# Gated sum of attention and a channel MLP: maxima's pieces, square roots, first weights and the order of units are moved

## The chip, the cores and the metric

The kernel runs on one core of a Trainium2 chip. The metric is device time in microseconds of one launch; smaller is better. The engines are TensorE (PE for its matmuls, PEld for its weight loads), VectorE (DVE), ScalarE (ACT), GpSimd (POOL) and SyncE (SP, which only issues DMAs). ACT issues some DMAs too, in its own instruction stream; in the profile "ACTq" and "SPq" are the DMA-issuing instructions of these two.

## What is computed

```python
def _A_ref(x, wqkv, wo):          # S=2048, D=512, H=32 heads of 16, window W=256
    q, k, v = split(x @ wqkv)
    scores = q @ k.T * (Dh ** -0.5)              # per head
    scores = where(0 <= i - j < W, scores, -1e9)
    return (softmax(scores) @ v) @ wo

def _B_ref(x, w1, b1, w2, b2):    # F=1792
    y = (x - mean(x)) / sqrt(var(x) + 1e-5)
    return gelu(y @ w1 + b1) @ w2 + b2

g = sigmoid((x * gate_w).sum(-1, keepdims=True))
out = g * _A_ref(A_x, A_wqkv, A_wo) + (1 - g) * _B_ref(B_x, ...)
```

In the kernel both branches start from arrays of the inputs given; everything is float32. Matmuls are made of two parts each: a value is split into a high part (rounded to the type fp32r) and a low part (the difference), and three products are summed: high by high, high by low, low by high.

## The kernel before, in words

The work has three stages.

**First stage: projections (the loop over `units`, 48 of them).** A q/k unit (`qk_unit`, matmuls on L288) makes 128 rows of q or k for 512 tokens in 12 matmuls; a v unit (`v_unit`, L313) makes v for 128 tokens in 12 matmuls, four by each of the three products. `first_units` makes the first two q/k units (L275) while their weights and inputs arrive in pieces. After a q/k unit, `qk_out` copies the result with ACT (a high part), subtracts it on DVE (a low part, L119, the helper `lo_part`), and both parts are written to DRAM: the high part by DMAs that ACT issues (L298), the low part by SP one step later (L299). Results of units sit in four PSUM buffers `d`.

Each unit is one step. `plan` holds what is put ahead of which unit: `at(n, fn)` puts `fn` ahead of unit n, and `after(k, fn)` defers to k steps later (`tick` runs these first). In the plan are, among others: the split of the weights Wv (`load_wv`; unit 6 is the first that needs it), the split of x chunk 3 (ahead of unit 6, its low parts on POOL), the weights of the next groups of heads (`load_w`: loaded at one step, split three steps later by an ACT copy and a DVE subtraction), the loads of stacks (below), and the statistics of the MLP branch: `stat_unit` loads 128 rows of x with SP (L434) and three steps later takes mean, variance and the gate's dot product on DVE (L438 to L440); `stat_end` (ahead of units 22 and 30, for half of the tokens each) takes 1/sqrt(var + eps) by an integer first guess and four Newton steps on [128, 8] tiles (L451 to L458), transposes the result (L461) and stores it to DRAM (L462). `load_y` reads it back (L481), loads x transposed (L489), and normalises on POOL (L492, L493: two operations of 128x512 for each of eight pieces).

**Maxima and attention.** q and k of four heads are loaded back as "stacks" (`load_stacks`, L324, two DMAs of 196 KB for 256 tokens; stack p holds heads 4p to 4p+3 in two pairs). An S unit (`s_pair`, L337) makes scores of a pair of heads for 128 queries, and DVE takes each query's maximum (L346 copies the masked block, L347 reduces). After four blocks of queries the maxima of both pairs are put back into the stacks as extra rows, so that the second product subtracts them. This way (`put_max`) has four pieces: `parts` (POOL splits into high and low part, L358 and L119), `turn` (DVE transposes, L362), `put` (SP stores to a DRAM tile `md`, L365), `rest` (SP loads them into the rows of `qk`, L371, which waits for the store's landing). A T unit (`st_pair`, L392) makes scores transposed for 128 keys, ACT takes exp (L394), POOL masks (L396). A P unit (`pv`, L411) multiplies by v.

**Second stage: attention and the MLP's first product, by the written order.** `ORDER` is a string of 1202 letters. T, S and P run the next unit of their kind; f runs the next two matmuls of the MLP's first product (`fill`, L611, no dependence on attention). The string is written out by a planner beforehand; the kernel only follows it. `spot[0]` counts the letters. In this stage the four pieces of a group's maxima are issued at `CHAIN` letters after the S unit that ends the group: (6, 11, 13, 20). In the first stage they follow by steps instead. A T unit at an even block of keys also issues the load of the next stack (`block`). Scores, P results and MLP results share four pairs of PSUM banks in turn (`two`, `ring`).

**Third stage: output.** The MLP's second product (`mlp2`, L821), the attention's output projection (L800) and the gates g0 and g1, which are exp, plus one, reciprocal (L466 on ACT, L470 and L471 on DVE, at the end of `stat_end(1)` in the kernel before).

Every engine runs its instructions in program order, and an instruction that waits holds those behind it. DMAs are issued by SP in program order too.

Of the kernel before, what the change touches and what calls it, by code (L numbers as in the profile page):

```python
# [13 lines left out]
F32R = mybir.dt.float32r  # L14
# [3 lines left out]
ALU = mybir.AluOpType  # L18
# [6 lines left out]
DT = D // 128  # L25
KT = D // 64
# [8 lines left out]
EPS = 1e-5  # L35
NEG = -3.0e38
U8 = mybir.dt.uint8
ORDER = ("fTSTffffffSffTfSfffTfSffTfSfffTSffffSPffSfffTSfffTfSffTfSfffTfffTSfTfffSffSPTTSPTSfffTfSffTfSfffTSff"
         "fTfSfffTSfffTfTfffSPSTTPfTSfTfffSffTfSfffTSfffTfSfffTfSffSPfSffSPfTfTSffTfSfffTSfffTfSffTfSfffTSfffT"
         "ffSfSPTSTPSTSPTSTfffSfTSfffTfSPTSffTffTfSffTfSfffTSffTfffSTPSTSPSTfTfffTSffTffSffTSffffTSfffTfSfffTS"  # L40
         "fffSPSTSPTTSTSPSfffTSfffTfSffTfTfffSffTfSfffTSfffTfSfPSTSPTSfSfffTffSffTfSfTffSffTfSfffTSfffTfSffSPS"
         "TSPfTfTSfffTfffTSfTfffSffTfSfffTSfffTfSffSPSTSPfTfSfTffSfffTSfffTffTffTSffTfSfffTfSffSPSTSPTffTSffTf"
         "fSffTfSfffTSfffTffTfSfTfffSfTPSfSPTTSPTfSfffTSfffTfSffTfSfffTSfffTfSffTfSfffSPTTSPSTffSfffSPTfSTfffT"
         "ffTSffTffTffTSffTfTfffSfSPTSTffTffTSffTffSffSPTfSfTffSfffTSfffTffSfTPfSTPSTSPfSTfffTfSfTffSffTfSfffT"
         "SfffTfSffTfSfffSPSTTPfTSfTfffSffTSffffTSfffTfSfffTffTfSfffSPSTSPfTffTfTSfffTfSffTfSfffTSfffTfSffTfSf"
         "ffSPTSPSfffTSfffTfSffTfSfffTSfffTfSfffSffSTffPTSSPfSfffTSfffTfSffTfSfffTSfffTfSffTfSfffSPTSffTffTffT"
         "SffTffTfSPfTSPTSffTffTffTSffTfSfffSPSTTPfTSfTfffSffTSffffTSffPfTSffTffSffTSffffSPSfTfSffffSTfffTffST"
         "fffTfSfTffSffTfSfffSPSTSPfTffTSffTfffTfSfTffSfffTSffffTSffffTSfPSTSPffTfTfSffTfffTfTSffffTSffTfSfffT"
         "SfffSfPTSTPTSPSffTSfffTfTffSfTffSfffTfSfffTSfffTffSfSPTfffTTPTffTfTfffTTfPfTTPTffTfTfffTfTffTfPfTTPf"
         "TT")  # L50
LAG = 6
CHAIN = (6, 11, 13, 20)


@with_exitstack
def gated_mix_kernel(ctx, tc: tile.TileContext, xt, x2, wqk, wv, wo, xa, gw, w1, w2, b1, b2, out):
    nc = tc.nc
    dve, act, pool, pe, sp = nc.vector, nc.scalar, nc.gpsimd, nc.tensor, nc.sync
# [18 lines left out]
    def get(key, tag, bufs, shape, dt=F32):  # L77
        return left[key].tile(list(shape), dt, name=nm(tag), tag=tag, bufs=bufs)
# [3 lines left out]
    def t2(dt=F32, shape=(128, 512)):  # L82
        return get("work", "t", nt[0], shape, dt)
# [28 lines left out]
    def view(t, *ap, off=0):  # L112
        return bass.AP(tensor=t.tensor, offset=t.offset + off, ap=[list(x) for x in ap])

    def f32(t):
        return t.bitcast(F32)

    def lo_part(lo, src, hi, eng=dve):
        eng.tensor_tensor(out=lo, in0=src, in1=f32(hi), op=ALU.subtract)  # L119

    def copy(dst, src):
        act.activation(dst, src, AF.Copy)  # L122
# [4 lines left out]
    def after(k, fn):  # L127
        todo.setdefault(step[0] + k, []).append(fn)
# [17 lines left out]
    stat = dram.tile([2, 2, S // 2], F32, name="stat")  # L146
# [12 lines left out]
    g0 = consts.tile([128, NB], F32, name="g0")  # L159
    g1 = consts.tile([128, NB], F32, name="g1")  # L160
    mv = consts.tile([128, NB, 2], F32, name="mv")
    rt = consts.tile([128, 2, 2, NB // 2], F32, name="rt")
# [14 lines left out]
    def split(w, raw, both=False):  # L177
        if both:
            dve.tensor_copy(w[:, 0], raw)
        else:  # L180
            copy(w[:, 0], raw)
        lo_part(w[:, 1], raw, w[:, 0])
# [29 lines left out]
    def load_wv(dt):  # L212
        w, raw = get("work", "wv", DT, (128, 2, 512), F32R), t2()
        wvs.append(w)
        sp.dma_start(raw, wv[dt])
        return lambda: split(w, raw)

    def load_x(c):
        h, l = x8(), x8()
# [20 lines left out]
        return rest, hi, lo  # L240

    def first_units():
        ws, raws, os = [], [], []
        for t in range(2):
            w = wt()
            wq[0, t] = w
            ws.append(w)
            raws.append(t2())
        pieces = (slice(0, 128), slice(128, 256), slice(256, 512))
        for k in pieces:  # L250
            for t in range(2):
                act.dma_start(raws[t][:, k], wqk[0, t, :, k])
        _, hi, lo = load_x(0)
        idle = t2()
        dve.memset(idle, 0.0)
        idle = idle.bitcast(BF16)
        o = two()[:, 0]
        for _ in range(12):
            pe.matmul(o, idle[:, :128], idle[:, :512], start=True, stop=True)
        masks()  # L260
        loads()
        for t in range(2):
            os.append(ps("d"))
        for dt in range(DT):
            for t in range(2):
                if dt < 3:
                    k = pieces[dt]
                    copy(ws[t][:, 0, k], raws[t][:, k])
                    lo_part(ws[t][:, 1, k], raws[t][:, k], ws[t][:, 0, k])
                if t == 0:  # L270
                    hi(dt)
                    lo(dt)
            for n, (k, x) in enumerate(((0, xh[0]), (1, xh[0]), (0, xl[0]))):
                for t in range(2):
                    pe.matmul(os[t], ws[t][:, k, dt * 128:dt * 128 + 128], x[:, dt * C:dt * C + C],  # L275
                              start=dt == 0 and n == 0, stop=dt == DT - 1 and n == 2)
        rests[1]()
        rests[2]()
        for t in range(2):
            qk_out(0, t, 0, os[t])  # L280
# [164 lines left out]
    def stat_end(half):  # L445
        ve = small("ve", 2, (128, NB // 2))
        u = small("u", 2, (128, NB // 2))
        m = mv[:, half * 8:half * 8 + 8]
        r = rt[:, half, 1]
        ri = r.bitcast(I32)  # L450
        dve.tensor_scalar(ve, m[:, :, 1], EPS, None, op0=ALU.add)  # L451
        dve.tensor_scalar(ri, ve.bitcast(I32), 1, None, op0=ALU.logical_shift_right)
        dve.tensor_scalar(ri, ri, -1.0, float(0x5f3759df), op0=ALU.mult, op1=ALU.add)
        for _ in range(4):
            dve.tensor_tensor(out=u, in0=r, in1=r, op=ALU.mult)
            dve.tensor_tensor(out=u, in0=u, in1=ve, op=ALU.mult)
            dve.tensor_scalar(u, u, -0.5, 1.5, op0=ALU.mult, op1=ALU.add)
            dve.tensor_tensor(out=r, in0=r, in1=u, op=ALU.mult)  # L458
        dve.tensor_copy(rt[:, half, 0], m[:, :, 0])
        s = small("ms", 2, (128, 32))  # L460
        dve.transpose(s, rt.rearrange("p h a b -> p (h a b)"))  # L461
        sp.dma_start(view(stat, [32, 4], [128, 32], [1, 32]), s)  # L462
        if not half:
            return
        for g, sgn in ((g0, -1.0), (g1, 1.0)):
            act.activation(g, z, AF.Exp, scale=sgn)  # L466

        def gate():
            for g in (g0, g1):
                dve.tensor_scalar(g, g, 1.0, None, op0=ALU.add)  # L470
                dve.reciprocal(g, g)  # L471

        after(1, gate)

    ys = {}

    def load_y(cp, s0, s1, lag, eng, gap=2):
        mr = [t2() for _ in range(2)]
        for j in range(2):
            for e in range(2):  # L480
                sp.dma_start(mr[j][64 * e:64 * e + 64], view(stat, [0, 64], [1, C], off=cp * S + j * 2 * C + e * C))  # L481

        def one(s):
            if (cp, 0, s // 4) not in ys:
                for k in range(2):
                    ys[cp, k, s // 4] = x8()
            h, l = (ys[cp, k, s // 4][:, s % 4 * C:s % 4 * C + C] for k in range(2))
            x = t2()
            sp.dma_start(x, x2[cp, :, s * C:(s + 1) * C])  # L489

            def rest():
                eng.tensor_tensor(out=x, in0=x, in1=mr[0], op=ALU.subtract)  # L492
                eng.tensor_tensor(out=x, in0=x, in1=mr[1], op=ALU.mult)  # L493

            def fin():
                copy(h, x)
                lo_part(l, x, h)
                done.add(("y", cp, s))

            after(lag, rest)  # L500
            after(lag + 3, fin)

        for s in range(s0, s1):
            after(1 + (s - s0) * gap // 2, lambda s=s: one(s))
# [19 lines left out]
    rests = {}  # L524
# [20 lines left out]
    def at(n, fn):  # L545
        plan.setdefault(n, []).append(fn)

    for dt in range(DT):
        at(4 + dt // 2, rests["v"][dt])
    at(6, rests[3])  # L550
    for i in range(4):
        at((3, 5, 6, 8)[i], lambda i=i: pool.memset(vs[:, 4 * i:4 * i + 4], 1.0))
# [8 lines left out]
    at(30, lambda: stat_end(1))  # L561
    for n, (g, t) in enumerate((g, t) for g in range(1, NG) for t in range(2)):
        at((6, 7, 9, 10, 12, 13)[n], lambda g=g, t=t: after(3, load_w(g, t)))
    at(24, lambda: load_y(0, 0, KT, 3, pool))
    at(33, lambda: load_y(1, 0, KT, 3, pool))
    at(41, lambda: load_w1(0, dve))
    at(44, lambda: load_w1(1, dve))
    for qb in range(NB - LAG):
# [193 lines left out]
    b2s = get("work", "b2s", 1, (128, D))  # L762
    sp.dma_start(b2s, view(b2, [0, 128], [1, D]))

    for n in range(2):
        after(1 + 2 * n, lambda n=n: early_wo(2 * n))
    us = {}
# [132 lines left out]
```

## Time and profile before

| | us |
|---|---|
| median of 3 runs | 751.23 |
| lowest, highest | 748.43, 751.72 |
| the profiled execution | 748.36 |
| its span (first to last instruction) | 746.6 |
| PE busy / DVE / ACT / POOL | 705.5 / 481.2 / 370.4 / 280.8 |
| mean granted TensorE clock | 0.981 |

The stages end at about 174 us (the first f) and 540 us (the last). How to read the lines that follow: in a list of waits, "PE ps_x L337 <- DVE mx L347: 9.0, 4, 4.0" says that PE's instructions of L337 that write ps_x stood 9.0 us in total, 4 times, at most 4.0 us, until DVE's L347 was done. In a timeline a row has start, duration, engine, line, operation, output<-input, shapes, count, and in brackets the idle time of the engine ahead of it with what ended it. In a row of a group, after the bar: busy us, mean ns of one, idle us ahead of them.

### The profile page before, as it was taken

What the parts mean: (1) busy time and instruction counts of PE and PEld (TensorE: products, weight loads), DVE (VectorE), ACT (ScalarE), POOL (GpSimd) and SP (SyncE); (2) the same over time, 40 slices, a digit from 0 to 9 for tenths busy, and PEclk for the clock granted to TensorE, in tenths of its full rate; (3) what the DMA queues carried; (4) which work ended last, traced back from release to release, by engine and by line L of the source; (5) the groups of instructions that cost most, each with busy time, mean ns of one, the idle gap of its engine ahead of it and who ended that gap; (6) DMA issues with size and microseconds to landing.
All of it is one profiled execution on the core that took longest, in us unless ns stands there. A gap on an engine that the chain in (4) does not pass through costs nothing.

```text
span 746.6 us, 15926 instructions
## 1 busy us (share of the span) xinstructions
PE 705.5 (94%) x5740; PEld 548.0 (73%) x5740; DVE 481.2 (64%) x1006; ACT 370.4 (50%) x585; POOL 280.8 (38%) x613
## 2 busy tenths in 40 slices
PE   8699986999999979998999999998999999999997
PEld 5477765778776757776777767876677788888886
DVE  5317969867686857766777868775455744735553
ACT  5322112346767747675776666766662413324131
POOL 9130026783646636554755564746400000000000
PEclk9799998999999989999999999999999999999999
DMA  8999574765675865546666465534485444343531
GB/s 278 300 283 296 188 225 148 230 201 144 212 252 172 247 184 179 162 157 206 211 207 186 140 185 173 182 132 133 130 301 168 158 149 152 136 130 109 180 110 56
DMA packets 102965, 137.92 MB, mean 185 GB/s; under 512 B 13960, under 2 KB 54088, under 8 KB 102760
## 3 DMA queue, kind: packets, MB, share of 16 engines
q1 hardware_dynamic: 95544, 124.59, 53.7%
q10 hardware_dynamic: 7344, 12.32, 5.2%
q8 instruction: 46, 0.75, 0.4%
q14 instruction: 31, 0.25, 0.1%
HBM read 81.53 MB, written 54.30 MB: 182 GB/s over the span
## 4 chain that ended last, share of the span: by engine, by line
PE 74%; DMA 11%; DVE 6%; SPq 4%; ACT 2%; issue 1%; ACTq 1%; POOL 0%; DVEq 0%
PE ps_b L611 19%; PE ps_a L821 16%; PE ps_b L411 11%; PE ps_d L288 7%; PE ps_b L392 6%; PE ps_b L337 6%; PE ps_o L800 5%; PE ps_d L313 5%; DMA qk<-qk 4%; DMA t<-in_xa 2%; DMA qk<-md 1%; ACTq L298 1%; DMA v<-in_xt 1%; DMA md<-ms 1%; DMA hp<-t 1%
## 5 line engine op out<-in xcount | busy, mean ns | idle before, releaser
L611 PE MATMUL ps_b<-x,w 64*128 64x512 f32 x1344 | 216.4, 400 | 0.2
L396 POOL TENSOR_SCALAR_AFFINE_SELECT p<-p 128x256 f32<-128x256 f32 x344 | 131.7, 411 | 108.2 <-ACT p L394 97.6
L394 ACT ACTIVATE p<-ps_b 128x768 f32<-128x768 f32 (+2 forms) x184 | 137.5, 770 | 53.5 <-PE ps_b L392 49.7
L821 PE MATMUL ps_a<-x,t 128*128 128x512 f32 x648 | 154.7, 395 | 0.1
L347 DVE TENSOR_REDUCE mx<-ps_b 128x2 f32<-128x512 f32 x208 | 144.2, 693 | 7.1
L821 PEld LDWEIGHTS ps_a<-x,t 128*128 128x128 f32 x648 | 121.4, 188 | 30.3 <-DVE t L119 0.8
L611 PEld LDWEIGHTS ps_b<-x,w 64*128 64x128 f32 x1344 | 132.4, 188 | 12.7 <-issue 4.0
L346 DVE COPY_PREDICATED ps_b<-tri,ps_b 128x256 f32<-128x256 uint8 x208 | 88.5, 425 | 68.0 <-PE ps_b L337 51.6
L392 PE MATMUL ps_b<-qk 64*128 64x384 f32 (+5 forms) x512 | 90.0, 342 | 8.9 <-DMA qk<-md 8.7
L337 PE MATMUL ps_b<-qk 62*128 62x384 f32 (+3 forms) x472 | 85.6, 344 | 7.6 <-DMA qk<-qk 6.2
L288 PE MATMUL ps_d<-x,w 128*128 128x512 f32 x360 | 92.3, 409 | 0.0
L288 PEld LDWEIGHTS ps_d<-x,w 128*128 128x128 f32 x360 | 69.5, 195 | 18.3 <-issue 2.2
L411 PE MATMUL ps_b<-p,v 128*32 128x256 f32 (+1 forms) x1376 | 74.6, 329 | 0.7 <-ACT p L394 0.7
L122 ACT ACTIVATE t<-ps_b 128x256 f32<-128x256 f32 (+1 forms) x113 | 52.3, 489 | 42.0 <-PE ps_b L411 32.6
L392 PEld LDWEIGHTS ps_b<-qk 64*128 64x128 f32 (+1 forms) x512 | 51.8, 186 | 25.8 <-issue 14.3
L396 POOL TENSOR_SCALAR_AFFINE_SELECT x<-x 128x256 f32<-128x256 f32 x136 | 52.3, 411 | 42.3 <-ACT x L394 41.3
L394 ACT ACTIVATE x<-ps_b 128x768 f32<-128x768 f32 (+2 forms) x72 | 54.8, 777 | 18.5 <-PE ps_b L392 11.5
L337 PEld LDWEIGHTS ps_b<-qk 62*128 62x128 f32 (+1 forms) x472 | 47.5, 186 | 21.7 <-issue 11.0
L411 PEld LDWEIGHTS ps_b<-p,v 128*32 128x32 f32 x1376 | 38.7, 109 | 26.8 <-issue 3.3
L119 DVE TENSOR_TENSOR t<-t,t 128x512 fp32r<-128x512 f32 x70 | 48.5, 693 | 14.6 <-ACT t L122 10.9
L313 PE MATMUL ps_d<-wv,x 128*128 128x512 f32 x192 | 50.9, 417 | 6.6 <-ACT wv L122 6.6
L313 PEld LDWEIGHTS ps_d<-wv,x 128*128 128x128 f32 x192 | 38.6, 202 | 17.0 <-ACT wv L122 8.0
(78 smaller groups left out, 635.2 us busy)
## 6 DMA issues: line engine op xcount, KB each, us to landing
qk<-qk SPq DMA_DIRECT2D x112, 196.0 KB
t<-hp SPq DMA_DIRECT2D x56, 256.0 KB
hp<-t SPq DMA_DIRECT2D x52, 256.0 KB
qk<-t ACTq DMA_DIRECT2D x40, 256.0 KB
qk<-t SPq DMA_DIRECT2D x32, 256.0 KB
osc<-t SPq DMA_DIRECT2D x31, 256.0 KB
t<-in_w SPq DMA_DIRECT2D x28, 256.0 KB
w<-w SPq DMA_DIRECT2D x28, 256.0 KB
```

Of the source, the lines that this page charges most:

```text
L122: act.activation(dst, src, AF.Copy)
L288: pe.matmul(o, a[:, dt * 128:(dt + 1) * 128], b[:, dt * C:(dt + 1) * C], start=n == 0, stop=n == 11)
L313: pe.matmul(o, x[:, a:a + 128], wvs[dt][:, k], start=n == 0, stop=n == 11)
L337: pe.matmul(o[:, e, :n], qs[pr][r:k, qb * 128:qb * 128 + 128], ks[pr][r:k, t0:t0 + n], start=True, stop=True)
L346: dve.copy_predicated(o[:, :, :128], tri, o[:, :, 256:384])
L347: dve.tensor_reduce(m, o[:, :, :256], mybir.AxisListType.X, ALU.max)
L392: pe.matmul(o[:, e, :w], ks[pr][r:k, kb * 128:kb * 128 + 128], qs[pr][r:k, kb * 128:kb * 128 + w], start=True, stop=True)
L394: act.activation(pt[:, :, :w], o[:, :, :w], AF.Exp, scale=0.25)
L396: pool.affine_select(out=pt[:, :, a:a + 128], in_=pt[:, :, a:a + 128], pattern=[[0, 2], [sgn, 128]], base=b, channel_multiplier=-sgn, comp ...
L411: pe.matmul(a[32 * h:32 * h + 32, at:at + w], vs[:, kb, v:v + 32], pts[p, kb][:, h, fr:fr + w], start=n == 0, stop=n == len(parts) - 1, sk ...
L611: pe.matmul(o[:, e], w[kt // 4][r:r + 64, k, m:m + 128], y[r:r + 64, a:a + C], start=n == 0, stop=n == 23)
L821: pe.matmul(accs[c][b], x[:, b * 128:(b + 1) * 128], w, start=f == 0 and n == 0, stop=f == FT - 1 and n == 2)
```

## The change

- The pieces of the maxima's way are issued 6, 13, 17 and 28 letters after S, in place of 6, 11, 13 and 20.
- `ORDER` is another string of the same length with the same units: the least distance from an S that ends a group to the first T that needs its maxima is 41 letters (23 before), and from a stack's load to its first S 22, then 27 (19 before).
- In `stat_end` the four Newton steps and the copy of the mean run on POOL; the transpose follows two steps later and the store three. The gate's last two operations go to the beginning of the third stage.
- Wv's high part is cast by DVE ahead of unit 3, all four tiles, and its low part is taken ahead of unit 5. Before, ACT copied and DVE subtracted tile by tile, two tiles ahead of unit 4 and two ahead of unit 5.
- The first weights of two units arrive in three DMAs, each with both units' columns, into one tile of Wv's buffers; before in six, into two tiles.
- `load_y` stands ahead of units 26 and 35, before 24 and 33.

```diff
--- before.py
+++ after.py
@@ -35,21 +35,21 @@
 EPS = 1e-5
 NEG = -3.0e38
 U8 = mybir.dt.uint8
-ORDER = ("fTSTffffffSffTfSfffTfSffTfSfffTSffffSPffSfffTSfffTfSffTfSfffTfffTSfTfffSffSPTTSPTSfffTfSffTfSfffTSff"
...
+ORDER = ("TfSffSffffTSffffTSfffTfSffTfSfffTSfffSPTSTSffffTSfffTfSfPTSffSfffTSffTffTfSfTffffSTPSTSPSTfTfffTSfff"
...
          "TT")
 LAG = 6
-CHAIN = (6, 11, 13, 20)
+CHAIN = (6, 13, 17, 28)
 
 
 @with_exitstack
@@ -213,7 +213,7 @@
         w, raw = get("work", "wv", DT, (128, 2, 512), F32R), t2()
         wvs.append(w)
         sp.dma_start(raw, wv[dt])
-        return lambda: split(w, raw)
+        return lambda: dve.tensor_copy(w[:, 0], raw), lambda: lo_part(w[:, 1], raw, w[:, 0])
 
     def load_x(c):
         h, l = x8(), x8()
@@ -240,16 +240,15 @@
         return rest, hi, lo
 
     def first_units():
-        ws, raws, os = [], [], []
+        ws, os = [], []
         for t in range(2):
             w = wt()
             wq[0, t] = w
             ws.append(w)
-            raws.append(t2())
+        raws = f32(get("work", "wv", DT, (128, 2, 512), F32R))
         pieces = (slice(0, 128), slice(128, 256), slice(256, 512))
         for k in pieces:
-            for t in range(2):
-                act.dma_start(raws[t][:, k], wqk[0, t, :, k])
+            act.dma_start(raws[:, :, k], wqk[0, :, :, k].rearrange("t p n -> p t n"))
         _, hi, lo = load_x(0)
         idle = t2()
         dve.memset(idle, 0.0)
@@ -265,8 +264,8 @@
             for t in range(2):
                 if dt < 3:
                     k = pieces[dt]
-                    copy(ws[t][:, 0, k], raws[t][:, k])
-                    lo_part(ws[t][:, 1, k], raws[t][:, k], ws[t][:, 0, k])
+                    copy(ws[t][:, 0, k], raws[:, t, k])
+                    lo_part(ws[t][:, 1, k], raws[:, t, k], ws[t][:, 0, k])
                 if t == 0:
                     hi(dt)
                     lo(dt)
@@ -452,25 +451,23 @@
         dve.tensor_scalar(ri, ve.bitcast(I32), 1, None, op0=ALU.logical_shift_right)
         dve.tensor_scalar(ri, ri, -1.0, float(0x5f3759df), op0=ALU.mult, op1=ALU.add)
         for _ in range(4):
-            dve.tensor_tensor(out=u, in0=r, in1=r, op=ALU.mult)
-            dve.tensor_tensor(out=u, in0=u, in1=ve, op=ALU.mult)
-            dve.tensor_scalar(u, u, -0.5, 1.5, op0=ALU.mult, op1=ALU.add)
-            dve.tensor_tensor(out=r, in0=r, in1=u, op=ALU.mult)
-        dve.tensor_copy(rt[:, half, 0], m[:, :, 0])
+            pool.tensor_tensor(out=u, in0=r, in1=r, op=ALU.mult)
+            pool.tensor_tensor(out=u, in0=u, in1=ve, op=ALU.mult)
+            pool.tensor_scalar(u, u, -0.5, 1.5, op0=ALU.mult, op1=ALU.add)
+            pool.tensor_tensor(out=r, in0=r, in1=u, op=ALU.mult)
+        pool.tensor_copy(rt[:, half, 0], m[:, :, 0])
         s = small("ms", 2, (128, 32))
-        dve.transpose(s, rt.rearrange("p h a b -> p (h a b)"))
-        sp.dma_start(view(stat, [32, 4], [128, 32], [1, 32]), s)
+        after(2, lambda: dve.transpose(s, rt.rearrange("p h a b -> p (h a b)")))
+        after(3, lambda: sp.dma_start(view(stat, [32, 4], [128, 32], [1, 32]), s))
         if not half:
             return
         for g, sgn in ((g0, -1.0), (g1, 1.0)):
             act.activation(g, z, AF.Exp, scale=sgn)
 
-        def gate():
-            for g in (g0, g1):
-                dve.tensor_scalar(g, g, 1.0, None, op0=ALU.add)
-                dve.reciprocal(g, g)
-
-        after(1, gate)
+    def gate():
+        for g in (g0, g1):
+            dve.tensor_scalar(g, g, 1.0, None, op0=ALU.add)
+            dve.reciprocal(g, g)
 
     ys = {}
 
@@ -545,8 +542,9 @@
     def at(n, fn):
         plan.setdefault(n, []).append(fn)
 
-    for dt in range(DT):
-        at(4 + dt // 2, rests["v"][dt])
+    for k in range(2):
+        for dt in range(DT):
+            at(3 + 2 * k, rests["v"][dt][k])
     at(6, rests[3])
     for i in range(4):
         at((3, 5, 6, 8)[i], lambda i=i: pool.memset(vs[:, 4 * i:4 * i + 4], 1.0))
@@ -561,8 +559,8 @@
     at(30, lambda: stat_end(1))
     for n, (g, t) in enumerate((g, t) for g in range(1, NG) for t in range(2)):
         at((6, 7, 9, 10, 12, 13)[n], lambda g=g, t=t: after(3, load_w(g, t)))
-    at(24, lambda: load_y(0, 0, KT, 3, pool))
-    at(33, lambda: load_y(1, 0, KT, 3, pool))
+    at(26, lambda: load_y(0, 0, KT, 3, pool))
+    at(35, lambda: load_y(1, 0, KT, 3, pool))
     at(41, lambda: load_w1(0, dve))
     at(44, lambda: load_w1(1, dve))
     for qb in range(NB - LAG):
@@ -762,6 +760,7 @@
     b2s = get("work", "b2s", 1, (128, D))
     sp.dma_start(b2s, view(b2, [0, 128], [1, D]))
 
+    after(1, gate)
     for n in range(2):
         after(1 + 2 * n, lambda n=n: early_wo(2 * n))
     us = {}
```

More of the change, by code (lines that the diff above doesn't have):

```diff
@@ L37 @@
 U8 = mybir.dt.uint8
-ORDER = ("fTSTffffffSffTfSfffTfSffTfSfffTSffffSPffSfffTSfffTfSffTfSfffTfffTSfTfffSffSPTTSPTSfffTfSffTfSfffTSff"
[L39 to L49, printed above, removed]
@@ new lines @@
+ORDER = ("TfSffSffffTSffffTSfffTfSffTfSfffTSfffSPTSTSffffTSfffTfSfPTSffSfffTSffTffTfSfTffffSTPSTSPSTfTfffTSfff"
+         "TfSffTfSfffTSfffTfSffTfSfffSPSTSPTffTSffTffTffTSffSPSfffTSfffTSfffTSffTfSffSPTSfTfffTffTSffTffSfTfSf"
+         "ffTSfffTfSffTffSfSPSTTPTTSPSTSPfSffTfSfffTSfffTffSfTfTffffTSffTffSffSPSffTSfffTfSffTfSfffTSfffTffSfT"
+         "PSfTffTfffSTPSTSPSffTSffffTffTfSfTffSfffTSffffTSffTffSfPSTSPTfSffTfSfffTSfTfffTfSfTffSffTfSfffTSfffS"
+         "PTTSPSTSPTffTSfffTfSffTfSffTSfffTfSfffTSfffTffSfSPSPfTfTSfffTfSffTSffffTSfffTfSffTfSfffTSffPTSTPSfTS"
+         "ffffTSffTffSffSPSTfffTSfTfffTfSfTffffSTPSTSPfTfTSffffTffSffSPfTfSfTffSfffTSfffTfSffSPTSfTfffTffTSffT"
+         "fffTfTSffffTSffTSfffTfSffSPSTSPSffTSfffTfSffTPTSfTfffSfTfSfffTfSffTfSfffSPfSTffTffSfTffSfffTSffTffSf"
+         "fTPfSTPTSffTffSffSPfTfSTfffSfffTSfffTfffTSfTfffSffTSffffSPfTfTSffffTfSffTfSfffTfSfffTSfffTfSfffSPTST"
+         "PTSTPSfTfSffTfSfffTSfffTfSffSfPTSffTfffSTffTffSPfTSfffTfSffTfSfffTfSffTfSfffTSfffTfffSTPTSTPSTfSffff"
+         "TSfffTfSffTfSfffTSfffSPSfTffTfffSTPSTSPSffTSfffTfSfffTSfffTSffTfSfffTSfffTfSfPfSTPSfTffSfffTfSfTfffT"
+         "SfTfffSffTfSffTfSfffSPTTSPSTTfffffSTPTSffTffSffTfSfffTSfffTfSffTfSffSPTSffTffTffTfTfSfSPSffTfSffTfSf"
+         "ffTSfffTfSffSPTfSfTffSffTSfffTSfffSSfffTffffTffffTfTPPTTPTfTffTfTffffTfTffPfTTPTfTffTfTfffTffTfPfTTP"
```

## Prediction

> **What bounds the kernel now.** I read the page first, then the waits of PE, then those stretches in which PE stood still, and last the timeline around each.
>
> ```profile
> span 746.6 us, 15926 instructions
> ...
> PE 705.5 (94%) x5740; PEld 548.0 (73%) x5740; DVE 481.2 (64%) x1006; ACT 370.4 (50%) x585; POOL 280.8 (38%) x613
> ...
> PEclk9799998999999989999999999999999999999999
> ```
>
> PE is busy for 705.5 of 746.6 us, so 41 us are standstill. The digits 7 and 8 of PEclk say that the standstill also costs clock. The waits of PE name its causes (total, times, longest):
>
> ```profile
> PE ps_x L337 <- DVE mx L347: 9.0, 4, 4.0
> PE ps_b L392 <- DMA qk<-md: 8.7, 3, 4.5
> PE ps_d L313 <- ACT wv L122: 6.6, 2, 4.6
> PE ps_b L337 <- DMA qk<-qk: 6.2, 5, 2.5
> PE ps_d L275 <- ACT x L122: 1.6, 1, 1.6
> ```
>
> The five make 32.1 us, and the change touches all five. The stretches around the long stalls (width, PE busy, other engines, PEclk, DMA share, GB/s) give the clock's part:
>
> ```profile
> 24.50:40.70 16.20, 9.64 (x26) 7.02 (x26) 4.48 (x7) 6.45 (x13) 5.34 (x5) 0.68 0.92 268
> 108.90:120.50 11.60, 6.97 (x19) 5.15 (x19) 10.79 (x19) 2.38 (x6) 9.81 (x8) 0.71 0.76 257
> 125.80:134.20 8.40, 4.01 (x12) 2.81 (x12) 8.16 (x19) 1.23 (x2) 2.88 (x2) 0.80 0.62 176
> 267.40:277.50 10.10, 5.57 (x30) 4.99 (x31) 2.86 (x6) 2.33 (x3) 3.10 (x10) 0.66 0.53 159
> 517.90:523.00 5.10, 1.81 (x34) 1.12 (x36) 1.48 (x3) 1.12 (x2) 2.03 (x5) 1.00 0.51 186
> ```
>
> A clock of 0.68 over 16.2 us is 0.32 x 2 x 16.2 = 10.4 us at half speed. It starts while PE stands; some 7.4 us of it are matmuls, so 3.7 us are lost on top of 6.6 us of standstill: 10.3 us. Row two in the same way: 6.7 us at half speed, nearly all busy behind the stall, 4.6 + 3.2 = 7.8. Row three: 4.4 + 1.7 = 6.1. Row four: 4.5 + 2.75 = 7.3. The stall in row five, 3.3 us, cost no clock.
>
> **Part 1: first weights, Wv.**
>
> ```profile
> 0.80 4.27 ACTq L252 DMA_DIRECT2D t<-in_wqk  x6
> ...
> 7.28 6.08 PE L275 MATMUL ps_d<-x,w 128*128 128x512 f32 x24 [1.59 <-ACT x L122]
> ...
> 20.90 0.69 DVE L119 TENSOR_TENSOR t<-ps_d,t 128x512 fp32r<-128x512 f32 x1 [1.17 <-ACT t L122]
> ...
> 24.89 3.50 ACTq L298 DMA_DIRECT2D qk<-t  x2
> ...
> 28.44 1.15 ACT L122 ACTIVATE wv<-t 128x512 fp32r<-128x512 f32 x2 [3.58 <-DMA qk<-t]
> ...
> 29.12 1.32 PE L313 MATMUL ps_d<-wv,x 128*128 128x512 f32 x2 [4.56 <-ACT wv L122]
> ...
> 40.47 5.74 PE L288 MATMUL ps_d<-x,w 128*128 128x512 f32 x24
> ```
> ```profile
> L179 DVE CAST x<-t 128x512 fp32r<-128x512 f32 x4 | 2.1, 517 | 1.7 <-DMA t<-in_w 1.7
> ```
>
> Three issues instead of six free ACT some 2 us earlier (half of 4.27), but the first copy still needs both weight tiles and x. Bounds: 0 and the whole 1.6 us wait; I take 0.4, since the bytes are the same.
>
> ACT copied Wv only at 28.44, behind two slow issues of its own. In the changed program four casts on DVE stand right behind the subtraction at 20.90: 21.6 + 4 x 0.52 = 23.7, before PE wants them at 29.12 - 4.56 = 24.56. So 8 of the first v unit's 12 matmuls (5.74 / 24 = 0.24 us each) run until 26.5. The last four need the low parts. Those moved to step 5, behind a subtraction that waits for an ACT copy that can't start before 28.44: 28.44 + 0.6 + 0.69 = 29.7, then 0.69 each, so 30.4 to 32.5. That unit then ends at 32.7, and the next one at 35.7 with full clock, at 38.5 if the clock halves again, against 40.5 before: 2 to 4.8 us.
>
> A stall of 3.9 us remains in this place, and 3.76 and 4.0 us cost the clock in rows two and three. The Trainium skill ("TensorE: Matmul & The Clock Gate", Part 1) says that the clock falls after an idle window of about 3.4 us, in a free-running grid; the 3.3 us stall above that cost none agrees. By that rule this stall may halve the clock, and the part is worth the lower end.
>
> What is late next is DMA: the first 60 us move at 0.92 share in row one, and the second weights of the next group arrive like this:
>
> ```profile
> 52.33 0.63 ACT L122 ACTIVATE w<-t 128x512 fp32r<-128x512 f32 x1 [3.44 <-DMA qk<-t]
> ...
> 54.86 1.43 PE L288 MATMUL ps_d<-x,w 128*128 128x512 f32 x5
> ```
>
> The copy ends 1.9 us ahead of its matmuls, so PE can be ahead by 1.9 us for nothing and by more only as far as the earlier DMAs of this part bring transfers forward. I take 3.0 for Wv; 3.4 with the start (bounds 1.5 and 6). The first weights' new home is a Wv buffer whose next writer is the fourth cast; their last reader stands ahead of it in DVE's own order, so this costs nothing.
>
> **Part 2: square roots on POOL.**
>
> ```profile
> 84.30 0.17 DVE L451 TENSOR_SCALAR ve<-mv 128x8 f32<-128x8 f32 x1
> ...
> 88.24 0.21 DVE L461 STREAM_TRANSPOSE ms<-rt 128x32 f32<-128x32 f32 x1
> ...
> 103.11 0.69 DVE L438 BATCH_NORM_STATS2 st<-t 128x6 f32<-128x512 f32 x1 [2.91 <-DMA t<-in_xa]
> ...
> 116.41 1.23 DVE L451 TENSOR_SCALAR ve<-mv 128x8 f32<-128x8 f32 x1
> ...
> 118.95 1.27 POOL L492 TENSOR_TENSOR t<-t,t 128x512 f32<-128x512 f32 x1
> 119.05 1.19 DVE L455 TENSOR_TENSOR u<-rt 128x8 f32<-128x8 f32 x1
> ...
> 126.39 0.21 DVE L461 STREAM_TRANSPOSE ms<-rt 128x32 f32<-128x32 f32 x1
> ```
> ```profile
> L119 POOL TENSOR_TENSOR nm<-mx,nm 128x16 fp32r<-128x16 f32 x32 | 7.1, 221 | 2.7
> ```
> ```profile
> SPq L371 <- DMA md<-ms: 40.8, 25, 3.4
> ...
> SPq L462 <- DVE t L119: 11.5, 1, 11.5
> ```
>
> A chain of 20 tiny operations holds DVE for 3.9 us the first time (84.30 to 88.24) and for 10.0 the second (116.41 to 126.39), where an operation of 0.17 takes 1.19 while POOL works on 128x512. The S units' reductions queue behind it, which is the 9.0 us wait. SP waited 11.5 us for the first result with the loads of x behind it, and DVE then starved for 2.91 us. On POOL the 17 moved operations cost 0.22 plus some 0.07 of spacing, 4.9 us, hidden: the transpose follows two steps later (two units of about 3 us), SP's store three. DVE's in-order queue behind the transpose would pay if POOL were later than that. In the second half POOL has its normalisation (1.27 each, 16 of them) too, but load_y now starts two steps later, behind the last statistics. Of the 7.8 + 6.1 = 13.9 us I take 12 (bounds 5 and 13.9). The gate's four small operations go into the last stage, where DVE has room: nothing.
>
> The Trainium skill ("SBUF — State Buffer", Who interferes with whom) has DVE and GpSimd exclude each other at a shared port pair when both read two SBUF inputs. The 1.19 beside the 1.27 agrees. It also speaks against this edit, since 16 more POOL operations a half now hold that pair; by it DVE would lose up to 16 x 0.22 = 3.5 us each half, and the sum would be 7 us less at worst.
>
> **Part 3: pieces at 6, 13, 17, 28, and the order.**
>
> ```profile
> 173.65 0.34 PE L392 MATMUL ps_b<-qk 64*128 64x384 f32 x2
> ...
> 530.76 0.34 PE L392 MATMUL ps_b<-qk 64*128 64x128 f32 x4
> ```
> ```profile
> 267.71 1.38 SPq L371 DMA_DIRECT2D qk<-md  x2
> ...
> 271.94 0.69 PE L392 MATMUL ps_b<-qk 64*128 64x384 f32 x2 [4.54 <-DMA qk<-md]
> ```
>
> The letters of the order run from 173.65 to 530.76, 1202 of them in both strings: 0.297 us a letter. Counted in the strings: from the S that ends a group of four to the first T that needs its maxima, 23, 37, 37, 39 letters at the shortest before, 41, 42, 45, 46, 46 after. From a stack's issue (at a T) to its first S, before 19 to 24 in 10 places, after 22 once and 27 five times, then 29 and more. PE's waits for stacks fell where this was short.
>
> Need after the change: the last piece is in SP's queue at letter 28, 8.3 us behind S, and takes 271.94 - 267.71 = 4.2 us to reach PE: 12.5 us or 42 letters. The two shortest lie there, so 0.3 us if SP is on time. Before, SP stood 40.8 / 25 = 1.6 us at this piece for the store ahead of it; with 11 letters (3.3 us) between store and reload instead of 7 (2.1 us), most of that goes. The pieces move past the stores, stack loads and result stores in SP's queue that lie in those 8 letters, and these are served earlier. I leave 2.0 of 8.7 us. Stacks: 27 letters are 8.0 us against 5.6 to 7.1 us in the short places before; I leave 1.5 of 6.2. Clock: 2.75 becomes 0.75. Gain 6.7 + 4.7 + 2.0 = 13.4 (bounds 4 and 17).
>
> **Sum.** 3.4 + 12 + 13.4 = 28.8. The profiled execution took 748.4 us (span 746.6 and 1.8 around it); the runs' median is 751.2. 748.4 - 28.8 = 719.6; the median stood 2.9 above the profiled one, half of which I add: 721.
>
> **Rivals.** *Maxima stay the wait (14%).* If SP is as late at letter 28 as before at 20, the 8.7 us and their clock stay: 721 + 8.7 = 730. For: two distances have no slack. Against: 1.2 us more between store and reload.
>
> *DVE or DMA keep the first stage (12%).* DVE starves for in_xa again, or POOL holds it: 9 us of part 2 stay, 730. For: the 2.91 us wait. Against: SP's 11.5 us go.
>
> *Slower (4%).* The last maxima piece at letter 28, in its place in SP's queue, comes late at every group. With SP 5 us late each T needs 12.5 + 5 = 17.5 us, 59 letters; the 30 distances of the new order then lack 52 us in all. 748.4 - 15.4 - 4.7 - 8.7 + 52 = 772. It decides from about 4 us of lateness, where 30 us are lacking. Against: the mean wait is 1.6 us.
>
> *Nothing of note (6%).* The front is held by DMA and the new order's densest places fill PSUM's ring: 745 to 752.
>
> **How the numbers follow.** 64% for 721. Its own range: with every part at its upper bound 748.4 + 1.4 - 6 - 13.9 - 17 = 713; with parts 1 and 2 at the lower one and part 3 at 9.3, 748.4 + 1.4 - 1.5 - 5 - 9.3 = 734. The two rivals at 730 lie in that range too, so 712 to 736 holds 8 in 10. About 0.5%, 4 us, is what can be told from no change here. Faster by more: 64 + 14 + 12 = 90%; same 5%; slower 4% and 1% of the last rival: 5%.
>
> **What would show it.** Right: the wait of L337 for mx gone; SP's wait at L462 under 3 us; DVE without operations of 1.2 us on 128x8; L313's wait now for DVE's subtraction and about 4 us; PE's waits for qk<-md and qk<-qk together under 5 us; PEclk at 9 outside the front. Wrong: PE waiting at L392 in many groups (part 3), DVE waiting at its transposes for POOL (part 2), PE waiting for w at 45 to 55 us (part 1).

## The result, and the profile after

The changed kernel takes 720.81 us (median of 4 runs, 719.47 to 725.15) against 751.48 us for the kernel before (748.43 to 753.54): ratio 0.9605, 95% interval 0.9552 to 0.9658. The forecast was 721.0.

The page of the changed kernel's profile, its span, engines and clock:

```profile
span 719.9 us, 15913 instructions
...
PE 702.1 (98%) x5740; PEld 541.8 (75%) x5740; DVE 472.6 (66%) x977; ACT 366.5 (51%) x580; POOL 288.6 (40%) x647
...
PEclk9999999989999999999999999999999999999999
```

PE is now still for 17.8 us instead of 41 us. The list of PE's waits of the changed kernel (line numbers are one to three lower now):

```profile
PE ps_b L336 <- DMA qk<-qk: 4.0, 2, 3.0
PE ps_d L312 <- DVE wv L119: 2.6, 1, 2.6
PE ps_x L258 <- DVE t L254: 1.5, 1, 1.5
PE ps_b L336 <- DVE t L119: 1.3, 1, 1.3
```

The waits of PE for maxima (8.7 us, for qk<-md) and, in the first stage, for reductions (9.0 us, ps_x for mx) are gone but for 0.2 us. The Wv stall shrank from 6.6 to 2.6, stack loads from 6.2 to 4.0. The fourth row is new: a wait at the border between the first and the second stage.

By stages, from the first matmul of each: the second stage (first f) began at 173.3 us and now begins at 154.4; the third (first matmul of the MLP's second product) at 539.6 and now at 513.0; the spans are 746.6 and 719.9. So the first stage gave 18.9 us, the second 7.7, the third nothing. The prediction had 15.4 and 13.4. **The sum came out right because two misses had opposite signs**: that it fits is luck, not precision.

The front of the changed kernel, in its timeline:

```profile
6.26 6.47 PE L274 MATMUL ps_d<-x,w 128*128 128x512 f32 x24
...
19.57 1.43 DVE L216 CAST wv<-t 128x512 fp32r<-128x512 f32 x4
...
26.39 0.60 ACT L122 ACTIVATE t<-ps_d 128x512 fp32r<-128x512 f32 x1 [3.75 <-DMA qk<-t]
...
27.62 2.49 DVE L119 TENSOR_TENSOR wv<-t,wv 128x512 fp32r<-128x512 f32 x4
28.36 6.64 PE L312 MATMUL ps_d<-wv,x 128*128 128x512 f32 x16 [2.59 <-DVE wv L119]
...
34.84 5.74 PE L287 MATMUL ps_d<-x,w 128*128 128x512 f32 x24
```

The matmuls of unit 8 (counted from 0, as in the plan) begin at 34.84 instead of 40.47: 5.6 us ahead. That lead was 5.1 us at the tenth v unit (98.05 instead of 103.19), just ahead of the stalls behind the square roots, and 19.2 us at the twelfth, behind them.

The border of the stages, in the timeline of the changed kernel:

```profile
153.46 1.28 POOL L489 TENSOR_TENSOR t<-t,t 128x512 f32<-128x512 f32 x1
...
154.77 0.60 ACT L122 ACTIVATE t<-ps_d 128x512 fp32r<-128x512 f32 x1 [4.29 <-POOL t L489]
154.82 1.26 POOL L490 TENSOR_TENSOR t<-t,t 128x512 f32<-128x512 f32 x1
...
155.40 0.69 DVE L119 TENSOR_TENSOR t<-ps_d,t 128x512 fp32r<-128x512 f32 x1 [3.05 <-ACT t L122]
...
156.15 0.44 PE L336 MATMUL ps_b<-qk 62*128 62x384 f32 x2 [1.31 <-DVE t L119]
```

Read it from the bottom: PE waits for DVE, DVE for ACT, and ACT had stood 4.29 us because its queue holds a copy of a normalised piece that POOL had not finished. POOL was 95% busy (48.44 of 51 us) from 104 to 155 us. The same stretches in a view by windows (width, PE, PEld, DVE, ACT, POOL busy, clock, DMA share, GB/s):

```profile
104.00:155.00 51.00, 50.84 (x224) 39.25 (x222) 35.32 (x43) 17.70 (x31) 48.44 (x51) 1.00 0.73 228
```
```profile
153.70:164.10 10.40, 8.12 (x43) 5.73 (x43) 6.59 (x12) 5.39 (x9) 3.83 (x6) 0.67 0.47 128
```

In the second, PE stands 2.3 us, and the clock of 0.67 means 6.9 us at half speed, some 3.4 us of work lost: 5.7 us together, as much as the second stage gained less than predicted. Not all of the shortfall need be here: behind the 3.03 us wait for a stack the clock was 0.77 over the 7.4 us from 245.6 to 253.0 us, some 1.7 us of work lost. And the clock's part at the border is not paid each time, as e5 and e8 show below.

### The profile page after: what moved, and what is told of

Same layout as the page of the kernel before. It is cut to its first block, busy times and chain, and to the rows that moved or that the text cites. A ratio compares the mean times of both kernels' runs of the same rounds, so it can differ in the third digit from the quotient of the medians.

```text
span 719.9 us, 15913 instructions
## 1 busy us (share of the span) xinstructions
PE 702.1 (98%) x5740; PEld 541.8 (75%) x5740; DVE 472.6 (66%) x977; ACT 366.5 (51%) x580; POOL 288.6 (40%) x647
## 4 chain that ended last, share of the span: by engine, by line
PE 68%; DMA 12%; POOL 7%; DVE 4%; SPq 3%; ACT 2%; issue 2%; ACTq 2%; POOLq 0%; DVEq 0%
PE ps_b L609 21%; PE ps_a L820 16%; PE ps_b L410 12%; PE ps_b L391 7%; PE ps_b L336 6%; PE ps_o L799 6%; DMA qk<-t 3%; POOL t L489 3%; POOL t L490 3%; DMA qk<-qk 2%; DMA t<-in_xa 2%; ACTq L297 1%; ACT t L122 1%; DMA t<-in_wqk 1%; DMA wv<-in_wqk 1%
## 5 line engine op out<-in xcount | busy, mean ns | idle before, releaser
L336 PE MATMUL ps_b<-qk 62*128 62x384 f32 (+2 forms) x472 | 86.4, 349 | 6.3 <-DMA qk<-qk 4.0
L391 PE MATMUL ps_b<-qk 50*128 50x384 f32 (+5 forms) x512 | 91.1, 345 | 0.4 <-DVE mx L346 0.3
L287 PE MATMUL ps_d<-x,w 128*128 128x512 f32 x360 | 88.6, 397 | 0.0
L287 PEld LDWEIGHTS ps_d<-x,w 128*128 128x128 f32 x360 | 66.9, 188 | 17.2 <-issue 1.9
L122 ACT ACTIVATE t<-ps_b 128x512 f32<-128x512 f32 (+1 forms) x112 | 51.9, 490 | 42.2 <-PE ps_b L410 35.5
L391 PEld LDWEIGHTS ps_b<-qk 50*128 50x128 f32 (+1 forms) x512 | 51.7, 186 | 20.0 <-issue 5.8
L393 ACT ACTIVATE x<-ps_b 128x768 f32<-128x768 f32 (+2 forms) x72 | 55.1, 778 | 18.0 <-PE ps_b L391 13.9
L410 PEld LDWEIGHTS ps_b<-p,v 128*32 128x32 f32 x1376 | 39.1, 110 | 26.7 <-ACT p L393 3.7
L119 DVE TENSOR_TENSOR t<-t,t 128x512 fp32r<-128x512 f32 x70 | 48.5, 692 | 14.6 <-ACT t L122 11.6
L312 PE MATMUL ps_d<-wv,x 128*128 128x512 f32 x192 | 49.5, 406 | 2.9 <-DVE wv L119 2.6
L122 ACT ACTIVATE t<-t 128x512 fp32r<-128x512 f32 x16 | 10.1, 632 | 77.8 <-DVE t L787 39.4
```

The costliest lines, as they stand in the source:

```text
L287: pe.matmul(o, a[:, dt * 128:(dt + 1) * 128], b[:, dt * C:(dt + 1) * C], start=n == 0, stop=n == 11)
L312: pe.matmul(o, x[:, a:a + 128], wvs[dt][:, k], start=n == 0, stop=n == 11)
L336: pe.matmul(o[:, e, :n], qs[pr][r:k, qb * 128:qb * 128 + 128], ks[pr][r:k, t0:t0 + n], start=True, stop=True)
L391: pe.matmul(o[:, e, :w], ks[pr][r:k, kb * 128:kb * 128 + 128], qs[pr][r:k, kb * 128:kb * 128 + w], start=True, stop=True)
L393: act.activation(pt[:, :, :w], o[:, :, :w], AF.Exp, scale=0.25)
L410: pe.matmul(a[32 * h:32 * h + 32, at:at + w], vs[:, kb, v:v + 32], pts[p, kb][:, h, fr:fr + w], start=n == 0, stop=n == len(parts) - 1, sk ...
```

## The experiments

The kernel before had, in the jobs below, medians of 750.7, 750.9 and 750.2 us. All ratios are to the kernel before in the same job (751.48 us for the first row). The stage times are those of the one profiled execution.

| kernel | median us | ratio (95% interval) | first f, third stage, span |
|---|---|---|---|
| the changed kernel | 720.81 | 0.9605 (0.9552 to 0.9658) | 154.4, 513.0, 719.9 |
| e1_front_alone | 742.94 | 0.9895 (0.9864 to 0.9927) | 169.0, 535.4, 741.3 |
| e2_roots_alone | 740.59 | 0.9873 (0.9828 to 0.9918) | 157.4, 529.4, 737.5 |
| e3_order_alone | 736.35 | 0.9813 (0.9772 to 0.9854) | 176.6, 531.3, 738.0 |
| e4_roots_dve_late | 726.79 | 0.9672 (0.9633 to 0.9711) | 167.3, 519.3, 726.1 |
| e5_old_chain | 722.45 | 0.9639 (0.9578 to 0.9700) | 153.9, 513.3, 720.1 |
| e6_norm_split | 716.04 | 0.9546 (0.9484 to 0.9608) | 153.7, 505.0, 710.4 |
| e7_low_step4 | 722.13 | 0.9632 (0.9579 to 0.9685) | 153.6, 515.3, 721.8 |
| e8_chain_wide_gap | 721.69 | 0.9616 (0.9561 to 0.9671) | 153.3, 509.6, 716.6 |
| f4_changed_again | 721.74 | 0.9611 (0.9572 to 0.9650) | 154.5, 511.5, 717.9 |
| f3_norm_split_again | 714.05 | 0.9514 (0.9472 to 0.9555) | 153.5, 506.0, 712.5 |
| f1_split_wide | 715.89 | 0.9534 (0.9498 to 0.9571) | 153.6, 507.2, 712.8 |
| f2_six_transfers | 723.04 | 0.9633 (0.9592 to 0.9674) | 156.0, 515.6, 721.5 |

My theory was that the three parts act in three places and add up, apart from the border; the rivals were that a lead is given back later (to DMA, or to the stalls behind the roots), or that DVE's hunger for x, and not the Newton chain, made the first stage's stalls.

**The parts, one at a time.** e1: the kernel before with the diff's `load_wv` and `first_units`, and

```diff
-    for dt in range(DT):
-        at(4 + dt // 2, rests["v"][dt])
+    for k in range(2):
+        for dt in range(DT):
+            at(3 + 2 * k, rests["v"][dt][k])
```

> The kernel before with part 1 alone (first weights in three DMAs, Wv cast by DVE). Theory (the parts act in different places and add up): unit by unit the changed kernel was 5.6 us ahead after the front, so this one is 5 to 6 us faster (ratio 0.992 to 0.993) and the stalls at L337 behind the square roots and the waits for qk<-md stay as before. Rival (the front is held by DMA, and PE's lead is given back at the next loaded weights or at the square roots): under 2 us.

It gained 7.8 us (750.74 to 742.94), more than the 5 to 6 expected, though the interval reaches down to 5.5. The second stage began 4.3 us earlier (169.0 against 173.3); in the profiled execution the stalls behind the roots were 10.0 us instead of 9.0. So the front's lead is kept, and the rival that DMA takes it back falls.

e2: the kernel before with the diff's `stat_end`, `gate` and `load_y` steps.

> The kernel before with part 2 alone (Newton steps on POOL, transpose and store later, load_y two steps later, the gate in the last stage). Theory: the 13.9 us of stalls and clock behind the square roots go, but POOL then runs without a break up to the end of the first stage and PE waits there, 2 us and up to 3.4 us of clock: 8 to 14 us faster (ratio 0.981 to 0.989). Rival (DVE starved for its x loads, which the change does not touch): L337's wait for mx stays above 4 us and the gain is under 5 us.

It gained 10.2 us (750.74 to 740.59), inside the expected 8 to 14. The trace splits it: the second stage begins 15.9 us earlier (157.4 against 173.3) and is 5.7 us longer (372.0 against 366.3). Its list of PE's waits has no row for mx in ps_x any more, and the new one of the border:

```profile
PE ps_b L392 <- DMA qk<-md: 7.7, 3, 5.5
...
PE ps_b L337 <- DVE t L119: 2.2, 1, 2.2
```

e3: the kernel before with the diff's `ORDER` and `CHAIN`.

> The kernel before with part 3 alone (pieces at 6, 13, 17, 28 and the new order). Theory: without the POOL chain at the stage's border the second stage gains what the prediction said, 12 to 15 us (ratio 0.980 to 0.984), of which the waits for qk<-md give 8.7. Rival (the new order is itself only worth what the changed kernel's second stage showed): 7 to 9 us.

It gained 14.4 us (750.74 to 736.35), with a second stage of 354.7 us, 11.6 us shorter than before. (The profiled execution was the slowest of its four, 739.73 us, and its first stage 3.3 us longer.) Here POOL ends its normalisation 9.5 us before the border (167.1 against 176.6 us), and the part is worth about what the prediction said. Its waits of PE, with no row left for qk<-md:

```profile
PE ps_x L337 <- DVE mx L347: 10.5, 5, 4.9
PE ps_d L313 <- ACT wv L122: 6.5, 2, 4.8
PE ps_b L337 <- DMA qk<-qk: 4.2, 2, 3.1
```

The three alone make 7.8 + 10.2 + 14.4 = 32.4 us; together they gave 30.7 (751.48 to 720.81). Within these intervals they add up.

**Which half of the roots' edit matters.** e4: the changed kernel with

```diff
-            pool.tensor_tensor(out=u, in0=r, in1=r, op=ALU.mult)
+            dve.tensor_tensor(out=u, in0=r, in1=r, op=ALU.mult)
```

and the other Newton operations and the copy of the mean likewise.

> The changed kernel with the Newton steps back on DVE; the later transpose, store, load_y and gate stay. Theory A (DVE's chain was the cost): the small operations take 1.2 us again beside POOL's normalisation, reductions queue, PE stalls 4 us or more at L336: slower than the changed kernel by 4 to 8 us, 725 to 729. Theory B (SP's store waiting on the chain, with x loads behind it, was the cost): within 2 us of it, or up to 5 us faster, since POOL ends its first stage 4.9 us earlier and PE's wait at the border goes: 716 to 722.

726.79 us, 5 to 6 us slower than the changed kernel (5 by the ratios, whose intervals just overlap; the changed kernel was not run in this job). The trace decides for theory A: the store was late and off SP's way in this kernel too, and PE stalled all the same. DVE's chain and PE's matmul in its timeline:

```profile
115.44 1.19 DVE L455 TENSOR_TENSOR u<-u,ve 128x8 f32<-128x8 f32 x1
...
122.65 0.69 PE L336 MATMUL ps_x<-qk 62*128 62x384 f32 x2 [7.17 <-DVE mx L346]
```

An operation of 0.17 us takes 1.19 again, and PE's single stall is 7.17 us, longer than the 4.0 before.

The chain is not behind both long stalls of the kernel before, though. The first of them, 4.00 us, ended at 112.95, and the second chain started at 116.41 only. What DVE stood for was a late load of x. These rows of the kernel before show SP's queue and then DVE (L481 and L371 are `load_y`'s and the maxima's reloads, L434 is the load of x):

```profile
96.93 3.88 SPq L481 DMA_DIRECT2D t<-stat  x4
...
100.85 1.56 SPq L371 DMA_DIRECT2D qk<-md  x2
...
104.18 0.58 SPq L434 DMA_DIRECT2D t<-in_xa  x1
...
109.41 0.69 DVE L438 BATCH_NORM_STATS2 st<-t 128x6 f32<-128x512 f32 x1 [2.85 <-DMA t<-in_xa]
```

In e4 `load_y` stands behind the last of these loads (SP issues it at 99.29 us, the last load at 98.58), and there is no long stall ahead of the one at 122.65, though the Newton steps are on DVE. So x loads held up in SP's queue, theory B's cause, made the first stall, and the chain the second. e1, with store and `load_y` in their old places, keeps both (4.01 and 5.08 us). But taking away the first alone gains little: PE comes earlier to the second and stands longer there. Whether the later store or the later `load_y` frees the first, no run separates.

The stage times show both sides of the edit: with the roots on DVE the first stage ends 12.9 us later (167.3 against 154.4), and the second is 6.7 us shorter (352.0 against 358.6): POOL ends its normalisation at 165.3, before PE reaches the border. Moving the roots is worth the difference of these two, 6 us.

**The border.** e6, and f3 once more beside the changed kernel itself:

```diff
             def rest():
-                eng.tensor_tensor(out=x, in0=x, in1=mr[0], op=ALU.subtract)
-                eng.tensor_tensor(out=x, in0=x, in1=mr[1], op=ALU.mult)
+                e = dve if cp and s % 2 else eng
+                e.tensor_tensor(out=x, in0=x, in1=mr[0], op=ALU.subtract)
+                e.tensor_tensor(out=x, in0=x, in1=mr[1], op=ALU.mult)
```

> The changed kernel with four of the eight pieces of the second load_y normalised by DVE instead of POOL (8 operations of 128x512). Theory (POOL's unbroken chain sets the end of the first stage): POOL ends it 10 us earlier, PE's stalls of 2.3 us at the border and the 3.4 us of clock behind them go: 715 to 717. Rival (DVE, which shares with POOL, becomes late in its place, so reductions queue): 720 or more, with PE waiting for mx at L336.

> The changed kernel with four pieces of the second normalisation on DVE, once more beside the changed kernel itself. Theory (POOL's unbroken chain cost 2.3 us of stall and 3.4 us of clock at the border of the stages): 4 to 7 us below it, ratio to the kernel before 0.952 to 0.955. Rival (its first time was chance): within 2 us of it.

> The changed kernel once more, as the measure for the three beside it: 718 to 723.

716.04 us, and in the direct comparison 714.05 us (712.31 to 715.94) against 721.74 (719.26 to 723.44): 7.7 us faster than the changed kernel, a little more than the 4 to 7 expected, and the ranges don't meet. The same window of f3, and the stretch at its border:

```profile
104.00:155.00 51.00, 51.00 (x230) 39.67 (x228) 40.83 (x55) 20.45 (x35) 38.48 (x43) 1.00 0.73 231
```
```profile
153.00:164.00 11.00, 9.79 (x93) 7.50 (x92) 10.53 (x22) 7.18 (x11) 4.80 (x14) 1.00 0.61 183
```

POOL's work fell by 10 us (48.44 to 38.48), DVE's rose by 5.5 (35.32 to 40.83), and the clock at the border stays 1.00, with PE standing 1.2 us still. The second stage takes 352.5 us instead of 357.1 beside it. That POOL's unbroken chain makes the loss at the border is shown, and that the split wins back 4.6 us; the rival, DVE late in POOL's place, falls. The profiled spans differ by 5.4 us (717.9 and 712.5), 1.0 of it in the first stage; the rest of the 7.7 us between the medians no trace shows.

How much the clock adds is not settled by the chain. f4, the same kernel again, has 2.2 us of standstill and a clock of 0.72 from 153 to 165 us. e5 and e8 below, with the same chain on POOL, stand 4.0 us (153 to 165) and 3.1 us (152.5 to 165) at a clock of 1.00.

**The pieces of the maxima's way.** e5: `CHAIN = (6, 11, 13, 20)` with the new order.

> The changed kernel with the pieces back at 6, 11, 13, 20; the new order stays. Theory (the distances in the order are what took PE's waits for maxima away; the later pieces are only room for SP): PE still does not wait at L391 for qk<-md, and the time is within 3 us of the changed kernel's 720.8. Rival (the later pieces are needed, because SP stands at the reload and holds the stack loads behind it): SP's wait for md<-ms grows from 44.6 to 60 us or more, PE's waits for qk<-qk grow by 4 us or more, 725 to 732.

722.45 us, within 1.7 us of the changed kernel. PE's wait for qk<-md stays away (0.2 us), and SP's wait at the reload is 45.9 us against 44.6: the rival falls. The wider distances in the order are enough to take PE's waits away; the later reload isn't needed. The later pieces with the old order were not run.

e8: `CHAIN = (6, 11, 13, 28)`.

> The changed kernel with pieces at 6, 11, 13, 28: store and reload 15 letters apart instead of 11. Theory (SP stands at the reload because the store's landing takes longer than the letters between them): SP's wait for md<-ms falls from 44.6 to under 25 us, stack loads are issued earlier, PE's wait for qk<-qk of 4.0 us shrinks: 716 to 720. Rival (SP is ahead of PE by no fixed distance, so it comes to the reload early whatever the gap): the wait stays above 38 us and the time stays within 1.5 us.

SP's wait at the reload did fall, from 44.6 to 31.8 us, between the two expectations, and PE's wait for stacks with it, to nothing in the list. The time did not: 721.69 us (718.40, the fastest of the four, in the profiled execution). The row of SP's waits, then PE's:

```profile
SPq L370 <- DMA md<-ms: 31.8, 18, 3.7
```
```profile
PE ps_b L391 <- DVE mx L346: 2.3, 4, 0.8
...
PE ps_b L336 <- DVE mx L346: 1.2, 2, 0.9
```

What came back is in DVE's waits. In the changed kernel and in this one, DVE's transpose waits for POOL's split:

```profile
DVE ms L361 <- POOL nm L119: 7.8, 8, 3.0
```
```profile
DVE ms L361 <- POOL nm L119: 16.2, 17, 3.0
```

With the transpose at letter 11, DVE stands 16.2 us for POOL instead of 7.8 at letter 13, and holds the reductions behind it. About 4.5 us of both are in the first stage, where letters don't count, so the second stage has 11.6 against 3.4. e5 and f1, with 11 too, have 15.9 and 15.3. So of the four numbers, the 13 has a visible effect in the traces, and the 28 as such none that can be measured in the time.

f1: both, the split and (6, 11, 13, 28).

> Both: the normalisation split and pieces at 6, 11, 13, 28. If SP's stand at the reload is what leaves PE's last waits for stacks, it falls to about 32 us as it did alone, those waits (2.6 us with the split alone) go, and the time is 1 to 3 us below the split alone. If what SP holds up is no longer waited for, it is within 1 us of the split alone.

715.89 us, 1.8 us above f3's 714.05 and so outside both expectations, though the ranges overlap; SP's wait was 27.0 us and that for stacks gone, and the 2.2 us at L391 for mx were there again. The lowest median is that of the changed kernel with the split alone.

**The front.** e7: `at(3 + k, ...)` in place of `at(3 + 2 * k, ...)`, so Wv's low parts come ahead of unit 4.

> The changed kernel with Wv's low parts taken ahead of unit 4 instead of unit 5. Theory: they no longer stand behind a subtraction that waits for ACT's slow issues, so PE's 2.6 us stall at L312 and 1.5 us of clock go: 717 to 719, if the lead is kept. Rival (DMA bounds the front): the stall moves to another wait ahead of 60 us, and the time stays within 1 us of 720.8.

722.13 us, outside the theory's 717 to 719. The stall at L312 went, and the time came back at the next thing that ACT does behind its slow issues, the copies of x chunk 3. This is the rival's moved stall; the row names ACT as what PE waits for, and whether DMA makes ACT's issues slow isn't shown:

```profile
30.71 2.19 ACT L122 ACTIVATE x<-v 128x512 fp32r<-128x512 f32 x4 [1.58 <-issue]
31.39 4.60 PE L287 MATMUL ps_d<-x,w 128*128 128x512 f32 x11 [1.82 <-ACT x L122]
```

PE reached the third v unit 0.8 us earlier than in the changed kernel (39.6 against 40.4) and the second stage at 153.6 against 154.4; its second stage then had two longer stalls, 3.10 us at the border and 3.97 us for a stack.

f2: the six transfers and two tiles of the kernel before, all else as changed.

> The changed kernel with the first weights in six transfers and two tiles again, Wv still cast by VectorE. Theory (the three transfers gave the 1.05 us by which the first matmul is earlier, and DMA does not take it back): first matmul at 7.2 us, PE ahead at the third v unit by 4.6 us instead of 5.6, time 1 us above the changed kernel. Rival (the front is held by DMA): the third v unit starts at the same time as in the changed kernel, within 0.3 us.

The first matmul starts at 7.31 us instead of 6.26, Wv's stall is 4.00 us instead of 2.47, and the third v unit starts at 42.3 against 40.9 in the changed kernel beside it. The third v unit is then 3.7 us ahead of the kernel before, where 4.6 was expected, and the second stage begins 1.5 us later than in the changed kernel (155.97 against 154.46). The medians, 723.04 and 721.74, can't be told apart. The trace decides for the theory: the earlier start isn't taken back by DMA in the front.

## Why the prediction came out right, step by step

- **Start: 0.4 us, measured 1.0.** ACT was free at 2.3 us, and the weights had landed at 5.35. The bounds (0 and 1.6) held.
- **Wv: 3.0 us, measured 4.6** (5.6 with the start; bounds 1.5 and 6). The mechanism is as told: casts on DVE in time, eight matmuls, then a stall for the low parts. Two sizes were off. The four casts took 1.43 us, not 4 x 0.52; and ACT's copy ahead of the low parts came at 26.39, since ACT's issues moved forward with the start, where the prediction held it at 28.44. So the stall was 2.6 and not 3.9 us. The lead was not lost at the weights at 52 us.
- **Clock in the front.** The half-speed stretch fell from 10.2 to 3.4 us. In the second profile of the changed kernel (f4) it was 6.8 us, with nearly the same stall (2.47 us). That is 1.7 and 3.4 us lost, where the prediction had 0 or 2.8. It judged the clock by the length of the stall; here a stall of 2.6 us halved it, shorter than the 3.3 us that cost none before. Part 1 came in near its upper bound all the same, because the stall itself was shorter than forecast.
- **Roots: 12 us, measured 14.1 in the first stage** (5.1 ahead of them, 19.2 behind). All of the 13.9 went. The prediction put the whole 9.0 us wait down to reductions queued behind the chain; half of it, the stall up to 112.95, came before the second chain and behind late x loads. Its reason for these was misread: SP waited 4.5 us for the first half's result, the 11.5 us are the second half's and came after DVE had starved. e4 shows the chain on DVE as the cause of the second stall, and that the other steps of the edit free the first but gain little without moving the chain: 12.9 of the 14.1 us came back. The 7 us that were conceded to POOL's hold on DVE did not come: the 17 operations ran in 5.1 and 4.6 us, and DVE's wait behind them was 1.5 us in the first half and 2.4 in the second.
- **"4.9 us, hidden": this step failed.** The prediction asked who waits for the transpose and the store, and not what else was queued behind the roots on POOL: 30 normalising operations of 1.3 to 1.7 us, and ACT's and DVE's work on their results at the end of the stage. Before, POOL had slack there (35.9 us busy of 51 in the same window): it ended its normalisation at 164.9 us, and PE reached the border at 173.3. Now PE arrives 18.9 us earlier and POOL, with the roots in its queue, only 8.8 us earlier (156.1). It cost 5.7 us in this profile, of which f3 wins back 4.6. The later `load_y` is probably part of it: POOL's first normalising operation began 2.7 us behind the tenth v unit's first matmul before, and 5.9 us behind it now. That share was not tried by itself.
- **Order: 13.4 us, measured 11.6 to 14.4 alone (e3), and 7.7 in the changed kernel**, the border's 5.7 included. Of its terms: the waits for maxima fell to nothing (2.0 left expected), the waits for stacks to 4.0 (1.5 expected). The largest of these, 3.03 us at 245.7, stood at a distance of 37 letters: SP issued that stack about 5 us late, at 240.93, behind a store and its reload, and PE had it at 248.68.
- **"Most of SP's 1.6 us at the reload goes": wrong.** 44.6 us in 24 waits, 1.9 us each. Moving store and reload both, by 4 and 8 letters, did not take SP off the store's landing; e8, with 15 letters between them, brought it to 31.8 us in 18 waits.
- **The sum**: +2.2 in the front, +2.1 at the roots, -5.7 in the second stage, and 0.5 us of the front's lead lost between the third and the tenth v unit. From span to span the gain is 26.7 us, where the terms made 28.8. That gives 748.4 - 26.7 = 721.7; the 1.4 us added for the distance between the profiled execution and the median cover most of the rest. That the median, 720.81, lies within 0.2 us of the forecast is luck in this too: it stood 0.8 us below the profiled execution (721.59) and not above it. The rivals with 730 and 772 did not occur, nor did the one at 745 to 752.

## What to carry to other kernels

An edit that speeds PE up to a border can make the slowest of the other engines' queues the next limit there: ask of each engine when its queue runs dry, and not only whether the moved operations fit beside others. Work moved off one busy engine is worth the difference of what it frees and what it delays, and a profile with the move undone (e4) shows both at once. Where several numbers of a plan change together, undo them one by one: here the order's distances carried the gain that the later pieces seemed to explain. A wait's total is not one cause: look at when each of its stalls ended and what the engine waited for stood behind.

## What the runs showed of the hardware

- In these runs the length of a stall does not decide whether the clock halves. At the changed kernel's border PE's stalls were 1.31, 0.60 and 0.36 us, and the clock was 0.67 over 10.4 us; in e8 they were 1.28, 0.60, 0.36 and 0.89 us at a clock of 1.00, and in e5 2.10, 0.61, 0.36 and 0.89 us, also at 1.00. In the kernel before, a single stall of 3.3 us cost none. What decides, the runs don't show.
- An operation of 128x8 on DVE takes 0.17 us alone. In a chain beside POOL's operations of 128x512, 6 of 20 (before) and 10 of 20 (e4) took 1.12 to 1.23 us, some with a single input among them, and the others 0.17. On POOL the same operations take 0.20. Four casts of 128x512 took 1.43 us on DVE with POOL at rest.
- The store of 16 KB to DRAM and its reload held SP 1.9 us a time in the mean in the changed kernel, at most 3.5.
